# Linear attention and experts on one core: a shared tile for the last 64 keys of two heads, elementwise work moved to GpSimd, and a new order of stages

## The chip, the cores and the metric

The kernel runs on one core of one Trainium2 chip. The metric is the device time of one execution in microseconds (us), from its start to its end. The text names the engines as the profile does: PE is TensorE's matmul, PEld its weight load, DVE VectorE, ACT ScalarE, POOL GpSimd, SP the engine that only issues DMAs.

## The reference

```python
def phi(x):                                   # (4, 8, 576, 64) -> (..., 256)
    proj = np.einsum('bhsd,df->bhsf', x, w_phi)          # 128 features
    proj = proj - np.max(np.abs(proj), axis=-1, keepdims=True)
    return np.concatenate([np.exp(proj), np.exp(-proj)], axis=-1)
q_p, k_p = phi(q), phi(k)
kv = np.einsum('bhsf,bhsd->bhfd', k_p, v)
z = np.sum(k_p, axis=2)
x = np.einsum('bhsf,bhfd->bhsd', q_p, kv) / (np.einsum('bhsf,bhf->bhs', q_p, z)[..., None] + 1e-6)
# x as (2304 tokens, 512); then 4 experts, all tokens through all of them
p = domain_probs / (domain_probs.sum(-1, keepdims=True) + 1e-09)
out = sum(p[:, e:e+1] * (np.maximum(x @ w1[e], 0) @ w2[e]) for e in range(4))   # 512 -> 1024 -> 512
```

## The kernel before

**Attention.** The 4 x 8 heads are worked on as 16 pairs of heads (two heads of one batch element). The features of keys are made with the keys as rows (`proj`, L289), their largest absolute value is subtracted (`proj_sub`), ScalarE takes both exponentials (`k_exp`), and `k_kv` (L358) multiplies them with the values into one bank, 66 columns for each of two heads and two signs, of which 65 are the values and a column of ones (for z). The 576 keys of a head are four tiles of 128 and one of 64. In that last tile each head is a step of its own: of the 128 rows 64 are keys and the other 64 are set to zero after the exponentials; the projection takes both heads side by side (256 columns), and four value products follow. Most matmuls run on numbers split into a high and a low part (fp32r), three products each; `k_kv` runs in plain fp32 at two instructions a product.

For pairs 4 to 15 ("stack") the queries take another path: high and low part stand stacked in the 128 rows (`split_pair`, L195 and L196), `q_proj` (L222) gives the features transposed, `q_max` (L237) takes block maxima on VectorE, which go through `max_d` in DRAM and come back broadcast as `mb`; `q_sub`, `q_exp2` and `q_lo` follow. `q_num` (L440) multiplies with the sums of `k_kv`; the denominators go through DRAM (`den_out`, `den_in`, `den_recip`, `rec_out`), come back broadcast as `rb` (`rec_in`, L479), and `x_mul` (L489) forms the x product. `x_out` splits it for the experts (L382, L502), `x_store` sends what comes later to `xd`.

**Experts.** 16 weight units (an expert's 256 hidden columns each) are run three times. The first time (`first_units`, L716 and `l2_tile`, L680) covers 512 tokens and is interleaved with the attention of pairs 4 to 15. The second and third time (`strassen_unit`, L886) cover 1024 and 768 tokens with seven products in place of eight on half-size blocks; the widths are 512 and 384 columns. These need sums of weight blocks (`s_sums`, L616 to L619, in tile `ws`), split into `s_hi` (L635) and `s_lo` (L643), and sums of token blocks (`x_ops`). Bank A is copied by ScalarE (L832) after the first product and written again by the fourth. Each unit's second layer runs during the next unit, its result added to `out` by VectorE (L690). Weights are loaded into two buffers `wraw` and split (`w_hi` L600, `w_lo` L606).

**What sets the order.** Every stage is a function in one queue that is sorted by a key. The lists `OLD` (pairs 0 to 3) and `NEW` (pairs 4 to 15) give each stage's key; pair i adds 16 i. `tick()` in the expert loops moves a clock forward by one step and emits what is due; `after(steps, fn)` puts something in relative to that clock. So the keys fix the order of instructions on each engine and nothing else: an engine that waits holds up what stands behind it. `FIRST` is the key 85 at which `first_units` starts, `LAST` that of the last `x_out`.

Of the kernel before, what the change touches and what calls it, by code (L numbers as in the profile page):

```python
# [20 lines left out]
def kernel(  # L21
# [17 lines left out]
    P = 128  # L39
# [27 lines left out]
    FETCH = (12, 28, 40, 46)  # L67
    W_WAIT = (5.5, 4.0, 0, 3.5)
# [72 lines left out]
    def load_pair(i, what):  # L141
        s = pairs[i]
        b, hp = divmod(i, NP)
        t0 = b * S
        if what == "kq" and s.stack:
            k = ip_.tile([P, S + 64], F32, name="kr", tag="kr", bufs=2)
            nc.sync.dma_start(k, kq[b, hp][:, 0 : S + 64])
            q = ip_.tile([P, 2 * S], F32, name="qr", tag="kq", bufs=2)
            s.kq = [k, q]
            for r in (0, 64):  # L150
                to = q[r : r + 64].rearrange("p (h s) -> p h s", h=2)
                src = kq[b, hp].rearrange("(h p) s -> p h s", h=2)
                nc.sync.dma_start(to[:, :, S - 64 : S], src[:, :, S : S + 64])
                nc.sync.dma_start(to[:, :, 0 : S - 64], src[:, :, S + 64 : 2 * S])
            return
        if what == "kq":
            s.kq = [ip_.tile([P, 2 * S], F32, name="kq", tag="kq", bufs=2)]
# [12 lines left out]
        t4, t4z = (slice(0, 64), slice(64, P)) if s.stack else (slice(64, P), slice(0, 64))  # L170
        nc.gpsimd.memset(s.v[t4z, 4, :], 0.0)
        for h in range(2):
            src = vsrc[:, h * 64 : (h + 1) * 64]
            dst = s.v[:, :, h * (2 * KW - 64) : h * (2 * KW - 64) + 64]
            nc.sync.dma_start(dst[:, 0:4], src[0:512].rearrange("(t p) d -> p t d", p=P))
            nc.sync.dma_start(dst[t4, 4], src[512:S])
# [10 lines left out]
    def split_pair(i, what):  # L187
# [12 lines left out]
        sl = KSL if what == "k" else QSL  # L200
# [4 lines left out]
        else:  # L205
            both = ip_.tile([P, 2 * S], F32R, name="qhilo", tag="qs", bufs=1)
# [8 lines left out]
    def q_proj(i, part, h):  # L215
# [3 lines left out]
        ps = s.ps[part, h] = ps_att.tile([P, 512], F32, name="projT", tag="att")  # L219
# [48 lines left out]
    def q_exp2(i, part, h):  # L268
# [5 lines left out]
        s.qe[part, h] = exps(src, slice(0, P), 1, 512 if part == 0 else 320, True)  # L274

    def proj(i, what, c):
# [7 lines left out]
        ps = s.ps[what, c] = ps_att.tile([P, 512], F32, name="proj", tag="att")  # L284
        for j in range(2 if c < 2 else 1):
# [8 lines left out]
    def proj_sub(i, what, c):  # L294

        s = pairs[i]
        g = 4 if c < 2 else 2
# [40 lines left out]
    def k_exp(i, c):  # L338
        s = pairs[i]
        t4, t4z = (slice(0, 64), slice(64, P)) if s.stack else (slice(64, P), slice(0, 64))  # L340
        rows, g = (slice(0, P), 4) if c < 2 else (t4, 2)
        d = s.d["k", c][rows, : g * NF]
        s.ke[c] = exps(d.rearrange("p (g f) -> p g f", f=NF), rows, g, NF, False)
        if c == 2:

            nc.gpsimd.memset(s.ke[c][0][t4z, : 2 * g * NF], 0.0)

    def k_kv(i, c):
# [4 lines left out]
        if c == 0:  # L353
            s.kv = ps_kv.tile([P, 512], F32, name="kv", tag="kv")
        for j, t in enumerate(tiles):
            for n in range(4):
                h, e0 = n // 2, (4 * j + n) * NF
                nc.tensor.matmul(  # L358
                    s.kv[:, n * KW : (n + 1) * KW],
# [66 lines left out]
    def q_num(i, part, h):  # L426
# [79 lines left out]
    def x_store(i):  # L506
# [21 lines left out]
        (14.5, q_tr, (1, 0)), (15.2, q_exp, (1, 0)),
        (16, q_lo, (1, 0)),
        (14.55, q_tr, (1, 1)), (15.5, q_exp, (1, 1)),  # L530
        (16.05, q_lo, (1, 1)),
        (18.6, q_num, (0, 0)), (19.9, q_copy, (0, 0)),
        (21.5, q_num, (1, 0)), (22, q_copy, (1, 0)),
        (22.7, q_num, (1, 1)), (23.3, q_copy, (1, 1)),
        (26.2, den_out, ()), (29.8, den_in, ()), (31.2, den_recip, ()), (32.5, rec_out, ()),
        (34.7, rec_in, ()), (36.9, x_mul, ()), (40.5, x_store, ()), (37, x_out, ()),
    )
    NEW = (
        (-22.75, load_pair, ("kq",)),
        (-15.3, load_pair, ("v",)),  # L540
        (-10.5, split_pair, ("k",)),
        (-5.8, split_pair, ("q",)),
        (-0.7, proj, ("k", 0)), (-0.6, proj_sub, ("k", 0)), (2.7, k_exp, (0,)),
        (6.94, k_kv, (0,)),
        (0.52, proj, ("k", 1)), (2.55, proj_sub, ("k", 1)), (4.04, k_exp, (1,)),
        (11.24, k_kv, (1,)),
        (2.8, proj, ("k", 2)), (4.64, proj_sub, ("k", 2)), (8.74, k_exp, (2,)),
        (12.48, k_kv, (2,)), (12.48, kv_hi, ()), (14.03, kv_lo, ()),
        (2.01, q_proj, (0, 0)), (6.04, q_max, (0, 0)),
        (6.24, q_proj, (1, 0)), (6.24, q_max, (1, 0)),  # L550
        (7.19, q_proj, (1, 1)), (7.19, q_max, (1, 1)),
        (9.04, q_maxT, ()), (9.04, q_maxrow, ()), (9.89, q_maxout, ()), (10.44, q_maxin, ()),
        (11.88, q_sub, (0, 0)), (14.38, q_exp2, (0, 0)),
        (13.23, q_sub, (1, 0)), (16.63, q_exp2, (1, 0)),
        (16.45, q_lo, (0, 0)),
        (13.43, q_sub, (1, 1)), (19.9, q_exp2, (1, 1)),
        (17, q_lo, (1, 0)),
        (22.85, q_lo, (1, 1)),
        (24.95, q_num, (0, 0)), (26.65, q_copy, (0, 0)),
        (26.15, q_num, (1, 0)), (26.9, q_copy, (1, 0)),  # L560
        (26.24, q_num, (1, 1)), (26.94, q_copy, (1, 1)),
        (30.24, den_out, ()), (31.27, den_in, ()), (32.22, den_recip, ()), (35.58, rec_out, ()),
        (36.98, rec_in, ()), (37.55, x_mul, ()), (44.4, x_store, ()), (39.37, x_out, ()),
# [45 lines left out]
    def s_sums(n):  # L609
# [5 lines left out]
        sub, tt = ALU.subtract, nc.vector.tensor_tensor  # L615
# [40 lines left out]
    def convert(kind, n, wait):  # L656
# [3 lines left out]
        if kind == "w1" and n >= NU:  # L660
            for o, fn in ((wait[0], s_sums), (wait[0] + 0.5, s_hi), (wait[1], s_lo)):
# [59 lines left out]
    def first_units():  # L721
        pend = []
        for n in range(NU):
# [12 lines left out]
            l1_done(n, W_WAIT[2:])  # L736
# [5 lines left out]
            if pend:  # L742
                l2_done(n - 1, W_WAIT[2:])
# [70 lines left out]
    def strassen_unit(n, x, pend, hooks):  # L814
# [9 lines left out]
        load("w1", n + 2, 1)  # L824
        load("w2", n + 1, 7)
# [24 lines left out]
        def evacuate(i):  # L850
            if i == 0:
                copy("s1", "A")
            elif i == 1:
                after(0.5, add, "u2", "s1", "B")
            elif i == 2:
                copy("s5", "C")
            elif i == 3:
                a = banks["A"][:, :nt]
                relu(0, 0, a)
                after(0.5, lo, 0, 0, a)  # L860
            elif i == 4:
                add("u3", "u2", "D")
                after(1, c22)
                after(2, lambda: nc.scalar.activation(c["c22"], c["c22"], AF.Relu))  # L864
                after(2, lambda: relu(1, 1, c["c22"]))
                after(3, lambda: lo(1, 1, c["c22"], False))
            elif i == 5:
                add("c12", "u2", "C")
                after(0.5, lambda: relu(0, 1, c["c12"]))
                after(1.5, lambda: lo(0, 1, c["c12"]))  # L870
            else:
                add("c21", "u2", "D")
                after(0.5, lambda: relu(1, 0, c["c21"]))
                after(1.5, lambda: lo(1, 0, c["c21"]))
# [23 lines left out]
        l1_done(n, (0.5, 2))  # L898
# [3 lines left out]
        l2_done(n - 1, (0.5, 2))  # L902
# [3 lines left out]
    def second_units(pend):  # L906
        xs, ops = xa, None
        for n in range(NU, 3 * NU):
# [3 lines left out]
            if n == 2 * NU - 1:  # L912
                ops["t4"] = ops["T1"] + ops["t4"]
                for i, name in ((1, "T2"), (2, "t4"), (4, "T3"), (5, "B22"), (6, "T4")):
                    hooks[i] = functools.partial(spread, ops[name], 0.5, 0.5)
            if n == 2 * NU - 2:
                ops = x_ops(xb)
                spread(ops["t"] + ops["t3"], 2, 1.5)
            if n == NU + 3:
                x_load(xb, xb.first, xb.nt)  # L920
                for k in range(NP):
                    after(4 + k, nc.scalar.activation, x0_hi[:, k, : xb.nt], xb.raw[:, k, : xb.nt], AF.Copy)
                    after(
                        6 + k,
# [134 lines left out]
```

## Time and profile before

| what | value |
|---|---|
| median of 3 runs | 991.61 us (987.24 to 992.78) |
| the profiled execution | 991.64 us, span 989.9 us |
| PE busy | 955.9 us (97%), 4883 matmuls |
| DVE busy | 683.8 us (69%) |
| ACT busy | 455.5 us (46%) |
| POOL busy | 542.1 us (55%) |
| mean granted TensorE clock | 0.985 |

The span goes from the first to the last instruction on the core. Busy time of PE is modelled at its ends and counts a pipelined matmul until it is through, so the spacing of starts tells what a matmul costs in a row of them. A wait is named by the engine, the tile it would write, its line, and after the arrow what released it.

### The profile page before, as it was taken

What the parts mean: (1) busy time and instruction counts of PE and PEld (TensorE: products, weight loads), DVE (VectorE), ACT (ScalarE), POOL (GpSimd) and SP (SyncE); (2) the same over time, 40 slices, a digit from 0 to 9 for tenths busy, and PEclk for the clock granted to TensorE, in tenths of its full rate; (3) what the DMA queues carried; (4) which work ended last, traced back from release to release, by engine and by line L of the source; (5) the groups of instructions that cost most, each with busy time, mean ns of one, the idle gap of its engine ahead of it and who ended that gap; (6) DMA issues with size and microseconds to landing.
All of it is one profiled execution on the core that took longest, in us unless ns stands there. A gap on an engine that the chain in (4) does not pass through costs nothing. (4 is left out here: it accounts for less than half of the span.)

```text
span 989.9 us, 13384 instructions
## 1 busy us (share of the span) xinstructions
PE 955.9 (97%) x4883; PEld 824.9 (83%) x4883; DVE 683.8 (69%) x1027; ACT 455.5 (46%) x832; POOL 542.1 (55%) x391
## 2 busy tenths in 40 slices
PE   8998999899999998899999999999989999999998
PEld 7887888788878887688888888888878888888887
DVE  5464776876766778867666666667876667676764
ACT  4675666656656543434333333332434434343441
POOL 3554657575654456655455445544665575655651
PEclk9898999999999999999999999999999999999999
DMA  6444545445543343322121211211132222212111
GB/s 157 127 124 131 136 127 153 122 132 165 142 119 105 130 150 99 102 87 68 43 79 59 64 43 43 63 55 54 43 106 86 65 65 63 86 58 71 64 43 64
DMA packets 74641, 91.42 MB, mean 92 GB/s; under 512 B 35120, under 2 KB 37040, under 8 KB 74576
## 3 DMA queue, kind: packets, MB, share of 16 engines
q1 hardware_dynamic: 74496, 90.55, 31.2%
q8 instruction: 38, 0.62, 0.3%
q14 instruction: 27, 0.22, 0.1%
q10 hardware_dynamic: 80, 0.03, 0.0%
HBM read 83.01 MB, written 7.54 MB: 91 GB/s over the span
## 5 line engine op out<-in xcount | busy, mean ns | idle before, releaser
L690 DVE SCALAR_TENSOR_TENSOR out<-l,pr,out 128x512 f32<-128x512 f32 x270 | 199.7, 746 | 96.2 <-PE l L680 95.1
L680 PE MATMUL l<-w2hi,h_lo 128*128 128x512 f32 x576 | 226.8, 394 | 3.9 <-DVE out L690 3.8
L680 PE MATMUL l<-w2hi,h_hi 128*128 128x512 f32 x576 | 226.3, 393 | 0.0
L680 PE MATMUL l<-w2lo,h_hi 128*128 128x512 f32 x576 | 226.1, 392 | 0.0
L643 POOL TENSOR_TENSOR w1lo<-wraw,w1hi 128x512 fp32r<-128x512 f32 x64 | 79.8, 1267 | 92.9 <-ACT w1hi L635 55.1
L680 PEld LDWEIGHTS l<-w2hi,h_lo 128*128 128x128 f32 x576 | 108.7, 189 | 23.4 <-DVE out L690 5.8
L680 PEld LDWEIGHTS l<-w2hi,h_hi 128*128 128x128 f32 x576 | 108.3, 188 | 23.2
L606 POOL TENSOR_TENSOR w2lo<-wraw,w2hi 128x1024 fp32r<-128x1024 f32 x48 | 116.8, 2434 | 16.5 <-ACT w2hi L600 8.6
L680 PEld LDWEIGHTS l<-w2lo,h_hi 128*128 128x128 f32 x576 | 108.6, 188 | 17.5
L838 ACT ACTIVATE h_hi<-c 128x512 fp32r<-128x512 f32 (+1 forms) x96 | 55.0, 578 | 68.8 <-DVE c L835 67.7
L848 POOL TENSOR_TENSOR c<-u,s 128x512 f32<-128x512 f32 (+1 forms) x32 | 37.2, 1162 | 86.8 <-DVE u L835 86.8
L358 PEld LDWEIGHTS kv<-v,e 128*128 128x128 f32 x640 | 81.1, 199 | 3.4
L358 PE MATMUL kv<-v,e 128*128 128x66 f32 x640 | 79.7, 279 | 0.0
L643 POOL TENSOR_TENSOR s_lo<-ws,s_hi 128x768 fp32r<-128x768 f32 x32 | 59.1, 1846 | 33.6 <-ACT s_hi L635 33.6
L864 ACT ACTIVATE c<-c 128x512 f32<-128x512 f32 (+1 forms) x32 | 18.6, 580 | 125.0 <-POOL c L848 125.0
L332 POOL TENSOR_TENSOR elo<-e,ehi 128x640 fp32r<-128x640 f32 x24 | 42.7, 1780 | 49.5 <-ACT ehi L324 45.0
L845 POOL TENSOR_TENSOR h_lo<-c,h_hi 128x512 fp32r<-128x512 f32 (+1 forms) x32 | 37.6, 1176 | 40.2 <-ACT h_hi L838 40.2
L600 ACT ACTIVATE w2hi<-wraw 128x1024 fp32r<-128x1024 f32 x48 | 50.5, 1052 | 12.8 <-PE l L680 12.7
L635 ACT ACTIVATE s_hi<-ws 128x768 fp32r<-128x768 f32 x32 | 27.1, 848 | 62.6 <-DVE ws L619 62.6
L606 POOL TENSOR_TENSOR w1lo<-wraw,w1hi 128x1024 fp32r<-128x1024 f32 x16 | 40.1, 2506 | 25.1 <-ACT w1hi L600 25.0
L716 PE MATMUL l<-x_hi,w1lo 128*128 128x512 f32 x128 | 52.8, 412 | 1.0 <-ACT x_hi L382 1.0
L886 PE MATMUL A<-x_hi,w1lo 128*128 128x512 f32 (+1 forms) x128 | 47.7, 373 | 6.2 <-ACT s L832 3.7
(161 smaller groups left out, 2226.2 us busy)
## 6 DMA issues: line engine op xcount, KB each, us to landing
wraw<-in_w_dram SPq DMA_DIRECT2D x96, 512.0 KB
mb<-max_d SPq DMA_DIRECT2D x12, 576.0 KB
qr<-in_kq_dram SPq DMA_DIRECT2D x24, 256.0 KB
rb<-rec_d SPq DMA_DIRECT2D x32, 144.0 KB
out_dram<-out SPq DMA_DIRECT2D x18, 256.0 KB
v<-in_v_dram SPq DMA_DIRECT2D x32, 128.0 KB
kr<-in_kq_dram SPq DMA_DIRECT2D x12, 320.0 KB
xd<-rb SPq DMA_DIRECT2D x8, 288.0 KB
```

The costliest lines, as they stand in the source:

```text
L332: engine.tensor_tensor(lo[sl], e[sl], parts[0][sl].bitcast(F32), op=ALU.subtract)
L358: nc.tensor.matmul(s.kv[:, n * KW : (n + 1) * KW], lhsT=e[:, e0 : e0 + NF], rhs=s.v[:, t, h * KW : (h + 1) * KW], start=(c == 0 and j == 0 ...
L600: nc.scalar.activation(hi, raw, AF.Copy)
L606: nc.gpsimd.tensor_tensor(lo, raw, hi.bitcast(F32), op=ALU.subtract)
L643: nc.gpsimd.tensor_tensor(dst, src, hi.bitcast(F32), op=ALU.subtract)
L680: nc.tensor.matmul(ps, lhsT=l[:, f, j * P : (j + 1) * P], rhs=r[:, f, :], start=(f == 0 and k == 0), stop=(f == 1 and k == 2),)
L690: nc.vector.scalar_tensor_tensor(o, ps, p, o, op0=ALU.mult, op1=ALU.add)
L716: nc.tensor.matmul(banks[n, f], lhsT=l[:, ksl], rhs=r[:, k, :], start=(k == 0 and j == 0), stop=(k == NP - 1 and j == 2),)
L838: nc.scalar.activation(h[b][0][:, f, :nt], src, AF.Relu)
L845: nc.gpsimd.tensor_tensor(dst, src, hi.bitcast(F32), op=ALU.subtract)
L848: nc.gpsimd.tensor_tensor(temp("c22"), c["u3"], c["s5"], op=ALU.add)
L886: nc.tensor.matmul(ps, lhsT=l[:, k * P : (k + 1) * P], rhs=r[:, k, :], start=(k == 0 and j == 0 and not again), stop=(k == 1 and j == 2), ...
```

## The change

It touches four things. In pairs 4 to 15 the last 64 keys of both heads share one tile of 128 rows (head 0 above, head 1 below). These keys are no longer loaded into `k` but, by two more DMAs, as 128 more columns of the stacked `q` tile, once in the rows of the high part and once in those of the low part; `proj` takes the tile with the stacked weights in two matmuls of 128 columns, and the values of the tile are block-diagonal (two blocks of zeros), so that `k_kv` makes two products of 132 columns in place of four of 66. The columns of the sums change their order from head, sign to sign, head. Second, `x_mul` runs on GpSimd in place of VectorE, in all 16 pairs. Third, so do the four weight sums of `s_sums`. Fourth, nearly all keys of the two lists change, and in the second units the waits are given for each stretch of units (`S_...`, `XB_...`, `W_WAIT_A`) in place of fixed numbers. The diff, cut to its core:

```diff
-    FETCH = (12, 28, 40, 46)
-    W_WAIT = (5.5, 4.0, 0, 3.5)
+    FETCH = (12.4, 27.45, 41.5, 43)
+    W_WAIT = (3.6, 1.4, 0, 2.85)
+    W_WAIT_A = (0, 3.5, 0.4, 2)
+    S_LOAD = (1, 5.35)
+    S_EV = (0.5, 0.5, 1, 2, 2, 3, 0.5, 1.5, 0.5, 1.5)
+    S_EV_A = (0.35, 1.3, 1, 2, 2, 3, 1.3, 1.5, 0.5, 0.7)
+    S_DONE = (0.5, 1, 3.5, 0.5, 1.45)
+    S_DONE_A = (0.5, 1, 3.5, 0.5, 2)
+    S_DONE_B = (0, 1, 5, 0.5, 2.4)
+    S_DONE_C = (0, 1, 5, 0.5, 2)
+    XB_HOOK = (0, 1.3, 0.5, 1.3, 0.35, 0.5)
+    XB_SUM = (0.4, 2.85)
+    XB_X = (4.4, 6)
...
-            k = ip_.tile([P, S + 64], F32, name="kr", tag="kr", bufs=2)
-            nc.sync.dma_start(k, kq[b, hp][:, 0 : S + 64])
-            q = ip_.tile([P, 2 * S], F32, name="qr", tag="kq", bufs=2)
+            k = ip_.tile([P, S - 64], F32, name="kr", tag="kr", bufs=2)
+            nc.sync.dma_start(k, kq[b, hp][:, 0 : S - 64])
+            q = ip_.tile([P, 2 * S + P], F32, name="qr", tag="kq", bufs=2)
...
+                nc.sync.dma_start(tail, src[:, :, S - 64 : S])
...
+        if s.stack:
+            t4 = [slice(0, 64), slice(64, P)]
+            nc.gpsimd.memset(s.v[0:64, 4, KW : 2 * KW], 0.0)
+            nc.gpsimd.memset(s.v[64:P, 4, 0:KW], 0.0)
...
-            t = ip_.tile([P, 2 * S], F32R, name="qs", tag="qs", bufs=1)
+            t = ip_.tile([P, 2 * S + P], F32R, name="qs", tag="qs", bufs=1)
...
+        if s.stack and c == 2:
+            for k in (1, 0):
+                nc.tensor.matmul(ps[:, 0:NF], lhsT=s.q[:, 2 * S :], rhs=wst[k], start=(k == 1), stop=(k == 0))
+            return
...
-        g = 4 if c < 2 else 2
+        g = 4 if c < 2 else 1 if s.stack else 2
...
-        rows, g = (slice(0, P), 4) if c < 2 else (t4, 2)
+        rows, g = (slice(0, P), 4) if c < 2 else (slice(0, P), 1) if s.stack else (slice(64, P), 2)
...
-        if c == 2:
-            nc.gpsimd.memset(s.ke[c][0][t4z, : 2 * g * NF], 0.0)
+        if c == 2 and not s.stack:
+            nc.gpsimd.memset(s.ke[c][0][0:64, : 2 * g * NF], 0.0)
...
+        if s.stack and c == 2:
+            for sg in range(2):
+                nc.tensor.matmul(
+                    s.kv[:, 2 * sg * KW : 2 * (sg + 1) * KW], lhsT=e[:, sg * NF : (sg + 1) * NF],
+                    rhs=s.v[:, 4, :], start=False, stop=True, skip_group_check=True,
+                )
+            return
...
-            nc.vector.tensor_tensor(s.xt[sl], s.nd[sl, h, :], s.rb[sl], op=ALU.mult)
+            nc.gpsimd.tensor_tensor(s.xt[sl], s.nd[sl, h, :], s.rb[sl], op=ALU.mult)
...
-        (30.24, den_out, ()), (31.27, den_in, ()), (32.22, den_recip, ()), (35.58, rec_out, ()),
-        (36.98, rec_in, ()), (37.55, x_mul, ()), (44.4, x_store, ()), (39.37, x_out, ()),
+        (29.06, den_out, ()), (29.77, den_in, ()), (31.42, den_recip, ()), (33.91, rec_out, ()),
+        (38.29, rec_in, ()), (39.91, x_mul, ()), (44, x_store, ()), (40.15, x_out, ()),
...
-        sub, tt = ALU.subtract, nc.vector.tensor_tensor
+        sub, tt = ALU.subtract, nc.gpsimd.tensor_tensor
...
-        l1_done(n, (0.5, 2))
+        l1_done(n, done[:3])
...
-        l2_done(n - 1, (0.5, 2))
+        l2_done(n - 1, done[3:])
```

The lines of keys are from `NEW`; the other keys of both lists change in the same way. In `OLD`, `x_mul` goes from 36.9 to 38.07 and `x_out` from 37 to 39.52, so that pair 3's `x_out` (16 x 3 more) comes after `FIRST`.

## Rows read from the trace of the kernel before

**Rows 1.** The windows view, one row for each stage; columns after the span: busy us.
```profile
core 0: us, PE busy (x) PEld busy (x) DVE busy (x) ACT busy (x) POOL busy (x), PEclk, DMA share, GB/s
0.00:85.00 85.00, 74.55 (x465) 67.83 (x466) 46.38 (x89) 51.40 (x106) 39.20 (x49) 0.92 0.50 131
85.00:391.50 306.50, 293.63 (x1708) 256.63 (x1707) 223.07 (x332) 180.69 (x329) 178.33 (x114) 0.99 0.47 134
391.50:433.80 42.30, 38.06 (x157) 30.11 (x158) 35.51 (x44) 17.22 (x30) 27.28 (x19) 0.97 0.27 88
433.80:719.00 285.20, 285.20 (x1258) 235.83 (x1257) 195.35 (x283) 104.62 (x178) 148.16 (x101) 1.00 0.19 58
719.00:742.70 23.70, 21.16 (x95) 18.13 (x94) 17.14 (x24) 8.35 (x17) 14.36 (x12) 0.93 0.34 111
742.70:990.00 247.30, 243.25 (x1207) 216.37 (x1205) 166.30 (x259) 93.27 (x174) 134.79 (x100) 1.00 0.21 67
```
**Rows 2.** Waits of TensorE, 85 to 391.5 us: total us, times, longest us.
```profile
PE num L440 <- DVE bm L237: 5.5, 6, 2.3
```
**Rows 3.** Timeline of VectorE around 214 us: start, us, instruction and count.
```profile
213.06 2.80 DVE L489 TENSOR_TENSOR rb<-nd,rb 64x576 f32<-64x576 f32 x2
215.89 1.11 DVE L237 TRANSPOSE_TENSOR_REDUCE bm<-projT 128x16 f32<-128x512 f32 x2
```
**Rows 4.** Waits of TensorE, 391.5 to 742.7 us.
```profile
PE A L886 <- ACT s L832: 3.7, 2, 2.5
PE A L886 <- DVE h_lo L703: 2.5, 1, 2.5
```
**Rows 5.** Timeline of ScalarE around 826 us; in brackets the idle time before.
```profile
825.54 0.85 ACT L635 ACTIVATE s_hi<-ws 128x768 fp32r<-128x768 f32 x1 [2.17 <-DVE ws L619]
826.30 0.46 ACT L832 COPY s<-A 128x384 f32<-128x384 f32 x1
```
**Rows 6.** Timeline of TensorE around 222 us.
```profile
221.49 1.89 PE L358 MATMUL kv<-v,e 128*128 128x66 f32 x16
223.19 0.47 PE L680 MATMUL l<-w2hi,h_lo 128*128 128x512 f32 x1
```
**Rows 7.** Timeline of TensorE around 11 us.
```profile
10.51 1.08 PE L289 MATMUL proj<-wbd,kq 128*128 128x256 f32 x4
11.43 0.60 PE L408 MATMUL dT<-ident,d 128*128 128x128 f32 x4
11.86 0.34 PE L358 MATMUL kv<-v,e 128*128 128x66 f32 x2
```
**Rows 8.** Timeline of TensorE around 208 us.
```profile
208.44 0.28 PE L289 MATMUL proj<-wbd_hi,klo 128*128 128x256 f32 x1
...
208.80 0.40 PE L716 MATMUL l<-x_hi,w1lo 128*128 128x512 f32 x1
```
**Rows 9.** Groups by line and shape, whole run: busy us, mean ns | idle before.
```profile
L196 POOL TENSOR_TENSOR qs<-qr,qs 64x1152 fp32r<-64x1152 f32 x12 | 31.8, 2650 | 8.5 <-PE num L440 3.4 <-ACT qs L195 3.0 <-issue 1.6
```
**Rows 10.** Timeline of the SP queue around 213 us.
```profile
212.97 0.61 SPq L154 DMA_DIRECT2D qr<-in_kq_dram  x1
219.00 0.33 SPq L255 DMA_DIRECT2D max_d<-mrow  x1
```
**Rows 11.** Groups of VectorE, 742.7 to 990 us.
```profile
L618 DVE TENSOR_TENSOR ws<-wraw 128x256 f32<-128x256 f32 x14 | 20.2, 1444 | 0.0
...
L619 DVE TENSOR_TENSOR ws<-wraw,ws 128x256 f32<-128x256 f32 x14 | 13.4, 955 | 0.0
...
L617 DVE TENSOR_TENSOR ws<-ws,wraw 128x256 f32<-128x256 f32 x14 | 5.9, 425 | 0.5
L616 DVE TENSOR_TENSOR ws<-wraw 128x256 f32<-128x256 f32 x14 | 5.8, 416 | 0.0
```
**Rows 12.** Groups of GpSimd, 742.7 to 990 us.
```profile
L845 POOL TENSOR_TENSOR h_lo<-c,h_hi 128x384 fp32r<-128x384 f32 x15 | 15.4, 1024 | 17.9 <-ACT h_hi L838 17.9
...
L643 POOL TENSOR_TENSOR w1lo<-wraw,w1hi 128x256 fp32r<-128x256 f32 x14 | 12.9, 921 | 0.0
```
**Rows 13.** The windows view for one unit of 384 tokens.
```profile
805.32:820.98 15.66, 15.66 (x79) 13.97 (x78) 10.98 (x17) 6.38 (x13) 9.46 (x7) 1.00 0.21 68
```

More of the change, by code (lines that the diff above doesn't have):

```diff
@@ L156, in load_pair @@
         if what == "kq":
-            s.kq = [ip_.tile([P, 2 * S], F32, name="kq", tag="kq", bufs=2)]
+            s.kq = [ip_.tile([P, 2 * S + P], F32, name="kq", tag="kq", bufs=2)]
             parts = ((0, 2 * P), (2 * P, 4 * P)) if i == 0 else ((0, 4 * P),)
@@ L199, in split_pair @@
         raw = s.kq[0]
-        sl = KSL if what == "k" else QSL
+        sl = slice(0, S - 64) if s.stack else KSL if what == "k" else QSL
         n = sl.stop - sl.start
@@ L205, in split_pair @@
         else:
-            both = ip_.tile([P, 2 * S], F32R, name="qhilo", tag="qs", bufs=1)
+            both = ip_.tile([P, 2 * S + P], F32R, name="qhilo", tag="qs", bufs=1)
             hi, lo = both[:, :n], both[:, S : S + n]
@@ L218, in q_proj @@
         s = pairs[i]
-        ps = s.ps[part, h] = ps_att.tile([P, 512], F32, name="projT", tag="att")
+        ps = s.ps[part, h] = bank(i, ps_l1, "l1", "projT")
         for k in (1, 0):
@@ L273, in q_exp2 @@
             src = s.d["q"][:, h, 256:S].unsqueeze(1)
-        s.qe[part, h] = exps(src, slice(0, P), 1, 512 if part == 0 else 320, True)
+        s.qe[part, h] = exps(src, slice(0, P), 1, 512 if part == 0 else 320, s.split_num)
     def proj(i, what, c):
@@ L563 @@
-        (36.98, rec_in, ()), (37.55, x_mul, ()), (44.4, x_store, ()), (39.37, x_out, ()),
+        (-23.15, load_pair, ("kq",)),
+        (-14.46, load_pair, ("v",)),
+        (-6.83, split_pair, ("k",)),
+        (-6.49, split_pair, ("q",)),
+        (-1.17, proj, ("k", 0)), (-0.67, proj_sub, ("k", 0)), (1.05, k_exp, (0,)),
+        (7.09, k_kv, (0,)),
+        (-0.1, proj, ("k", 1)), (2.4, proj_sub, ("k", 1)), (7.84, k_exp, (1,)),
+        (12.44, k_kv, (1,)),
+        (3.05, proj, ("k", 2)), (3.84, proj_sub, ("k", 2)), (7.64, k_exp, (2,)),
@@ new lines @@
+        (12.48, k_kv, (2,)), (12.48, kv_hi, ()), (12.53, kv_lo, ()),
+        (1.39, q_proj, (0, 0)), (6.04, q_max, (0, 0)),
+        (6.24, q_proj, (1, 0)), (6.64, q_max, (1, 0)),
+        (7.04, q_proj, (1, 1)), (7.19, q_max, (1, 1)),
+        (9.04, q_maxT, ()), (9.04, q_maxrow, ()), (10.59, q_maxout, ()), (10.84, q_maxin, ()),
+        (12.03, q_sub, (0, 0)), (14.38, q_exp2, (0, 0)),
+        (13.18, q_sub, (1, 0)), (16.93, q_exp2, (1, 0)),
+        (16.6, q_lo, (0, 0)),
+        (12.48, q_sub, (1, 1)), (19.9, q_exp2, (1, 1)),
@@ L660, in convert @@
         if kind == "w1" and n >= NU:
-            for o, fn in ((wait[0], s_sums), (wait[0] + 0.5, s_hi), (wait[1], s_lo)):
+            wait = (wait[0], wait[0] + 0.5, wait[1]) if len(wait) == 2 else wait
+            for o, fn in zip(wait, (s_sums, s_hi, s_lo)):
                 later(max(clock.key, LAST + XA_LATE + 1) + o * clock.step, functools.partial(fn, n))
@@ L735, in first_units @@
                 tick()
[L736 removed]
+            l1_done(n, W_WAIT_A[:2] if n >= NU - 2 else W_WAIT[2:])
             if n:
@@ L853, in evacuate @@
             elif i == 1:
-                after(0.5, add, "u2", "s1", "B")
+                after(ev[0], add, "u2", "s1", "B")
             elif i == 2:
@@ L921, in second_units @@
                 for k in range(NP):
-                    after(4 + k, nc.scalar.activation, x0_hi[:, k, : xb.nt], xb.raw[:, k, : xb.nt], AF.Copy)
+                    after(XB_X[0] + k, nc.scalar.activation, x0_hi[:, k, : xb.nt], xb.raw[:, k, : xb.nt], AF.Copy)
                     after(
-                        6 + k,
+                        XB_X[1] + k,
                         lambda k=k: nc.vector.tensor_tensor(
```

111 lines of the change are left out of this document (49 added, 62 removed).

## The prediction

> **What bounds the kernel now.** I read the busy time of each engine by stage first [rows 1]. The stages are cut at what the trace shows: up to 85 us attention alone, to 391.5 us attention interleaved with the first expert units, to 433.8 us the start of the second units, to 719 us units of 512 tokens, to 742.7 us the change to 384 tokens, and from there units of 384. The reader is to see that TensorE is the bound nearly everywhere and how little idle time it has: 10.5 us before 85, 12.9 us in the interleaved stage (306.50 less 293.63), 4.2 us in the next (42.30 less 38.06), none in 433.8 to 719, 2.5 us around 719, and 4.1 us after, which I take for the tail behind the last matmul. The granted clock is below 1.00 only in stages with idle time. So the time falls in two ways: TensorE gets less to do, or the idle stretches close. 433.8 to 719 can give nothing.
>
> Second, what those stretches wait for. In the interleaved stage the largest item is the numerator matmul waiting for VectorE's block maximum, 5.5 us in six waits [rows 2]. The timeline of VectorE in one such place shows why [rows 3]: two x products take 2.80 us, from 213.06, and the block maximum that TensorE wants starts at 215.89, straight after them. From 391.5 to 742.7 two product-A matmuls wait 3.7 us for ScalarE's copy of A, and one 2.5 us for VectorE's h_lo [rows 4]. Behind that copy is a chain: ScalarE's s_hi waits for VectorE's last weight sum, and the copy stands behind it in ScalarE's order. In a steady unit of 384 the chain ends so: s_hi waited 2.17 us and started at 825.54, the copy at 826.30 [rows 5].
>
> **The change, part by part.** *Tail tile, values.* Each of 12 pairs loses half of its last four value products. Each of those is two instructions (fp32), so 8 become 4, twice as wide (132 columns for 66). Sixteen of the old kind start between 221.49 and 223.19, 0.106 us each [rows 6]. The trace has no 132-column one. From below it costs what a 66-column one does, 0.106: saved 4 x 0.106 = 0.42 us a pair. From above, four fp32 instructions of 256 columns take 10.51 to 11.43, 0.23 each [rows 7], so 132 columns in proportion 0.119: saved 8 x 0.106 less 4 x 0.119 = 0.37. I take 0.37, the nearer kind.
>
> *Tail tile, projection.* Three matmuls of 256 columns, 208.44 to 208.80, 0.36 us [rows 8], become two of 128. Half of 0.12 each is the lower bound, 0.06. The nearest row is the transpose of 128 columns: four between 11.43 and 11.86, 0.108 each [rows 7]. I take 0.108: saved 0.36 less 0.22 = 0.14 us; by the lower bound 0.24. Together 0.51 us a pair (0.66 at most), times 12 is 6.1 us (7.9). Pair 4 does this before 85 us, where TensorE has idle time to lose it in, so **5.6 us**.
>
> *The smaller work around it.* One memset of GpSimd a pair goes, the maximum and subtraction of the tail halve, ScalarE's exponentials of the tail have half the columns on twice the rows; the q split grows from 1152 to 1280 columns, the k split shrinks from 640 to 512. None of these engines is the bound, and their idle time hides it, so nothing is booked; uncovered, the q split would cost a ninth of 2.65 us, 0.3 us a pair [rows 9]. Two more DMAs a pair stand in SP's queue, 0.61 us each: the block-maximum store behind them would be 1.2 us late if SP were full, but SP is idle from 213.58 to 219.00 there [rows 10].
>
> *x products to GpSimd.* VectorE loses 2.80 us a pair just ahead of the block maximum. GpSimd has no such row; half of its 64x1152 subtraction, 2.65 us, gives 1.33 each [rows 9], 2.65 a pair. GpSimd is busy 178.33 of 306.50 us in that stage [rows 1]; a dozen pairs add some 32, 69% in all. What the move adds is a wait: on GpSimd the product stands in line behind the reciprocals' broadcast, with the low parts of the exponentials and splits queued behind it, and the numerator and projections wait for those. Bounds: at best the 5.5 us of waits go; at worst they come back as waits on GpSimd, nothing gained. I take **4.5 us**: the longest wait is 2.3 us against 2.80 removed, so all could close, and a new one or two are likely to remain.
>
> *Weight sums to GpSimd.* In a unit of 384, four sums leave VectorE, 3.2 us together [rows 11]. GpSimd's nearest row is a subtraction of the same 128x256 shape, 0.921 us [rows 12], so 3.7 us a unit. GpSimd is busy 9.46 of 15.66 us there [rows 13], and h_lo waits 17.9/15 = 1.2 us on ScalarE with nothing between [rows 12]: 9.46 + 3.7 + 1.2 = 14.4, which fits. The sums need nothing but the raw weights, so GpSimd can start them when it is through with the unit's h_lo; s_hi and the copy behind it come no later. In steady units TensorE has no idle time to win, so the gain is zero; it is paid for if the 14.4 grows past 15.66. The dearest row for a sum is VectorE's 1.444, while another of the same shape takes 0.416 [rows 11]: at 1.444 on GpSimd the unit would need 16.4.
>
> The Trainium skill explains such a pair of rows: "SBUF — State Buffer", section "Who interferes with whom", says that a VectorE instruction with two SBUF inputs and a GpSimd instruction that reads SBUF block each other for a whole instruction. By this rule a sum on GpSimd is free of the blocking and the forecast stands; were 1.444 what the operation itself costs, the sum would end 11 us later (rival C).
>
> *The two junctions* (391.5 and 719) lose 4.2 and 2.5 us idle, plus clock: a granted 0.97 over 42.3 us and 0.93 over 23.7 us is 1.3 and 1.7 us. Together 9.7 us. Sums off VectorE and new hooks may close part; but GpSimd, busy 27.28 of 42.30 in the first [rows 1], gets some three sets of sums, 11 us, and becomes nearly full. Bounds 0 and 9.7 gained; I take **2.5**, because the copy of A still stands behind s_hi and s_hi behind the sums.
>
> *Stages placed anew.* In 85 to 391.5 the order of matmuls against the other engines changes; the rows can't price it. Bounds: all 12.9 us close, or as many again open. I book no more than the 4.5 above. Before 85, pair 3's x product costs 2 x 1.33 ahead of the first expert matmuls that read it; its output is placed after three groups of them, which is cover. I book zero.
>
> Sum: 991.64 (the profiled execution, whose span is 989.9 with 1.7 outside it, and which is at the median of the runs, 991.61) less 5.6, 4.5 and 2.5 is **979 us**.
>
> **The rivals.** *A: only the work comes off.* VectorE's waits close and waits on GpSimd open in their place (the x product behind its broadcast), the junctions stay: 991.6 less 5.6 = 986, 982 to 990. For it: TensorE's waits add up from small ones of many kinds. Against: the largest kind has one cause, and that is removed.
>
> *B: the new order closes nearly all idle time.* 12.9, 4.2, 2.5 and the 3 us of clock, with 5.6 of work: 991.6 less 28 = 963. For it: nothing but order holds these waits. Against: each has another releaser.
>
> *C: GpSimd becomes the bound in the units of 384, slower.* The point from which it decides: a sum of (15.66 - 1.2 - 9.46)/4 = 1.25 us. At VectorE's dearest 1.444 each of 14 such units ends 4 x 0.19 us late, 11 us; GpSimd that late gives back no waits elsewhere either, so 991.6 less 5.6 plus 11 = 997. For it: 14.4 of 15.66 leaves little. Against: GpSimd's own row of this shape is 0.921, measured beside the very VectorE sums that leave. The Trainium skill's "GPSIMD Engine Reference", section "Engine selection", speaks for C: it advises VectorE for elementwise work, GpSimd being about twice as slow with two inputs; twice VectorE's mean of 0.81 would be 1.6 a sum and some 1007 us in all.
>
> *D: the wide value product costs twice the narrow one,* so that nothing is saved on it: 12 x 0.37 back, 983. Against it: 256 columns take 0.23, so 132 can hardly take 0.21.
>
> **How the numbers follow.** The forecast 979 (970 to 984) has 0.55, A 0.20, B 0.10, C 0.10, D 0.05. About half a percent, 5 us, is what a measurement can tell from no change: the runs shown go from 987.24 to 992.78. Faster means under 986.7. The forecast, B, D and most of A lie there, less a little for an order that misses: 0.79. Same: the rest of A and C's mild end, 0.12. Slower: the rest of C and an order that opens new waits, 0.09. The range from 964 to 990 leaves out half of B, most of C and the new waits.
>
> **What would show it.** Right: the tail's value products at 0.106 to 0.12 us with half as many; VectorE's block maximum no longer behind x products and the wait for it under 2 us in all; GpSimd some 13 us busy in a unit of 384, and that unit still 15.6 to 15.7 us; idle time in 85 to 391.5 of 6 to 10 us. Wrong: waits of TensorE on GpSimd's low parts above 5 us in that stage (A), a unit of 384 longer than 16 us (C), idle time under 4 us there (B), or a stage before 85 that grows or shrinks by more than 3 us, which I left at zero.

## The result, and the profile after

The changed kernel takes 966.79 us (median of 4 runs, 966.39 to 967.29) where the kernel before took 990.31 beside it (4 runs, 987.24 to 992.78): a ratio of 0.9764, 95% interval 0.9734 to 0.9795. It is faster by 23.5 us; 12.6 were forecast. The profiled execution is 967.29 us with a span of 965.5.

The windows view of the kernel after, with the columns of [rows 1]. Its stages are cut at five events: the first expert product, and the first product A of the first, third, 17th and 18th of the second units.

```profile
0.00:80.43 80.43, 69.32 (x448) 62.35 (x449) 38.83 (x79) 48.55 (x100) 45.91 (x53) 0.95 0.52 136
80.43:371.71 291.28, 286.16 (x1664) 250.49 (x1664) 197.23 (x311) 182.91 (x335) 208.24 (x144) 1.00 0.50 140
371.71:413.98 42.27, 38.81 (x157) 30.89 (x158) 26.94 (x32) 18.12 (x32) 37.32 (x31) 0.92 0.32 99
413.98:699.60 285.62, 285.62 (x1261) 236.57 (x1260) 160.82 (x227) 104.77 (x178) 190.36 (x156) 1.00 0.18 58
699.60:718.77 19.17, 18.66 (x91) 16.25 (x90) 13.66 (x19) 8.13 (x17) 15.92 (x16) 1.00 0.40 132
718.77:965.50 246.73, 242.96 (x1207) 217.45 (x1205) 125.92 (x203) 92.58 (x173) 169.28 (x154) 1.00 0.20 67
```

The first cut of [rows 1] lies 2.9 us behind its event and the cut at 719 lies 0.7 ahead. At exactly these events the kernel before has 82.09 us in the head (the stage up to the first expert product), 309.43 in the interleaved stage, then 42.25, 285.90, 22.97 and 247.20. Its first two:

```profile
0.00:82.09 82.09, 72.13 (x454) 66.06 (x455) 43.77 (x85) 48.52 (x100) 37.64 (x48) 0.92 0.50 130
82.09:391.52 309.43, 296.06 (x1719) 258.42 (x1718) 225.71 (x337) 183.56 (x335) 179.92 (x115) 0.99 0.47 134
```

So the head gave 1.7 us, the interleaved stage 18.2, the first junction (371.71 to 413.98) nothing, the units of 512 tokens 0.3, the second junction (699.60 to 718.77) 3.8, and the units of 384 0.5: together the 24.4 us by which the span fell. TensorE's idle time in the interleaved stage fell from 13.37 to 5.12 us. GpSimd took what VectorE lost: 208.24 busy us there, and 37.32 of 42.27 in the first junction.

The waits of TensorE in the interleaved stage:

```profile
PE l L715 <- DVE out L725: 3.1, 2, 1.7
PE l L751 <- POOL x_lo L536: 0.8, 1, 0.8
PE l L751 <- ACT x_hi L416: 0.4, 1, 0.4
PE maxT L264 <- DVE bm L256: 0.2, 1, 0.2
```

The numerator's 5.5 us of waits for the block maximum [rows 2] are gone, and no wait on GpSimd's low parts of the exponentials has come for them. The waits from 371.7 to 718.77, which answer to [rows 4]:

```profile
PE C L923 <- POOL B22lo L823: 2.3, 1, 2.3
PE C L923 <- ACT s L869: 1.2, 1, 1.2
PE A L923 <- POOL w1lo L677: 0.6, 1, 0.6
PE A L923 <- ACT s L869: 0.5, 1, 0.5
```

Here the waits changed hands: 6.2 us on ScalarE's copy and VectorE's low part (9.3 with the smaller waits of that stretch) have become 4.6, the longest on GpSimd.

TensorE's timeline at two places, the tail's value products and its projection, against [rows 6, 8]:

```profile
96.80 0.39 PE L392 MATMUL kv<-v,e 128*128 128x66 f32 x2
97.02 0.67 PE L383 MATMUL kv<-v,e 128*128 128x132 f32 x4
97.44 0.48 PE L751 MATMUL l<-x_hi,w1lo 128*128 128x512 f32 x1
...
127.86 0.33 PE L308 MATMUL proj<-wst,qs 128*128 128x128 f32 x2
128.03 0.45 PE L715 MATMUL l<-w2hi,h_lo 128*128 128x512 f32 x1
```

Read start to start, not by the duration: two instructions of 66 columns take 0.22 us, four of 132 take 0.42. Either kind costs 0.11 each. The two projection matmuls take 0.17 together.

The groups of GpSimd in the units of 384 (busy us, mean ns | idle before), against [rows 12]:

```profile
L651 POOL TENSOR_TENSOR ws<-ws,wraw 128x256 f32<-128x256 f32 x13 | 12.2, 942 | 1.0
...
L677 POOL TENSOR_TENSOR w1lo<-wraw,w1hi 128x256 fp32r<-128x256 f32 x14 | 10.4, 745 | 0.0
L653 POOL TENSOR_TENSOR ws<-wraw,ws 128x256 f32<-128x256 f32 x14 | 10.4, 744 | 0.0
L652 POOL TENSOR_TENSOR ws<-wraw 128x256 f32<-128x256 f32 x13 | 9.6, 737 | 0.0
L650 POOL TENSOR_TENSOR ws<-wraw 128x256 f32<-128x256 f32 x13 | 9.6, 737 | 0.0
```

The four sums take 942 + 744 + 737 + 737 = 3160 ns a unit, and one such unit by the windows view, against [rows 13]:

```profile
781.36:797.00 15.64, 15.64 (x80) 14.06 (x79) 8.04 (x13) 6.37 (x13) 11.93 (x12) 1.00 0.22 69
```

### The profile page after: what moved, and what is told of

Its sections match the earlier page's. It is cut to its first block, busy times and chain, and to the rows that moved or that the text cites. A ratio compares the mean times of both kernels' runs of the same rounds, so it can differ in the third digit from the quotient of the medians.

```text
span 965.5 us, 13190 instructions
## 1 busy us (share of the span) xinstructions
PE 941.5 (98%) x4823; PEld 814.0 (84%) x4823; DVE 563.4 (58%) x867; ACT 455.1 (47%) x832; POOL 667.0 (69%) x551
## 4 chain that ended last, share of the span: by engine, by line
PE 77%; POOL 6%; DMA 6%; DVE 4%; ACT 2%; issue 2%; SPq 2%; POOLq 0%; ACTq 0%
PE l L715 36%; PE C L923 8%; PE D L923 8%; PE A L923 8%; PE l L751 5%; PE B L923 4%; PE num L474 3%; PE kv L392 3%; PE proj L314 1%; DVE dq L285 1%; DMA mb<-max_d 1%; DMA wraw<-in_w_dram 1%; POOL w2lo L640 1%; POOL rb L523 1%; DMA qr<-in_kq_dram 1%
## 5 line engine op out<-in xcount | busy, mean ns | idle before, releaser
L357 POOL TENSOR_TENSOR elo<-e,ehi 128x640 fp32r<-128x640 f32 x24 | 40.1, 1673 | 52.9 <-ACT ehi L349 47.8
L392 PEld LDWEIGHTS kv<-v,e 128*128 128x128 f32 x544 | 65.5, 193 | 5.1 <-ACT e L345 2.4
L392 PE MATMUL kv<-v,e 128*128 128x66 f32 x544 | 66.0, 274 | 3.1 <-ACT e L345 1.5
L677 POOL TENSOR_TENSOR w1lo<-wraw,w1hi 128x512 fp32r<-128x512 f32 x64 | 65.2, 1040 | 0.0
L872 DVE TENSOR_TENSOR u<-s,B 128x512 f32<-128x512 f32 (+1 forms) x32 | 19.9, 621 | 64.4 <-ACT s L869 30.7
L523 POOL TENSOR_TENSOR rb<-nd,rb 64x576 f32<-64x576 f32 x32 | 46.7, 1458 | 8.0 <-DMA rb<-rec_d 6.7
```

What stands on the lines that cost most here:

```text
L357: engine.tensor_tensor(lo[sl], e[sl], parts[0][sl].bitcast(F32), op=ALU.subtract)
L392: nc.tensor.matmul(s.kv[:, o * KW : (o + 1) * KW], lhsT=e[:, e0 : e0 + NF], rhs=s.v[:, t, h * KW : (h + 1) * KW], start=(c == 0 and j == 0 ...
L523: nc.gpsimd.tensor_tensor(s.xt[sl], s.nd[sl, h, :], s.rb[sl], op=ALU.mult)
L677: nc.gpsimd.tensor_tensor(dst, src, hi.bitcast(F32), op=ALU.subtract)
```

## The experiments

The edits are named T (the tail tile), X (x products on GpSimd), W (weight sums on GpSimd), K (the keys of both lists, with `FETCH` and `W_WAIT`) and S (the waits given by stretch in the second units). No kernel leaves work out. A gain in us is the ratio's, of 990 us, unless medians are named; the two can differ by some 2 us (T alone is 7.1 faster by the ratio, 5.4 by the medians). Stage times are of each kernel's profiled execution, between the events above, and such a time varies for the same instructions. `ws` below changes nothing in the head, and in the interleaved stage at most the last weight sums. Its head:

```profile
0.00:79.59 79.59, 70.01 (x455) 63.29 (x455) 43.75 (x85) 48.40 (x100) 37.62 (x48) 0.96 0.52 135
```

That is 2.5 us less in the head, at a granted clock of 0.96 for 0.92, and its interleaved stage is 306.03 us, 3.4 less. In these two stages a difference of less than some 3 us is not told apart by one execution each.

### One part alone

T alone is the diff's hunks from `load_pair` to `k_kv`, with the new order of columns in `q_num`; all else is as before.

> The kernel before with the shared tail tile alone. Theory 1 (each gain is the part's own, as the prediction summed them): 5.6 to 6.1 us faster, value products of 132 columns at 0.11 to 0.12 us each. Theory 2 (the new order is what closes the idle time and the parts only fit into it): the matmul time falls by as much, but idle time of the old order opens in its place, so 0 to 4 us faster.

It takes 980.67 us, ratio 0.9928 (0.9897 to 0.9958): 7.1 us of 990. The interleaved stage is 299.96 us, TensorE busy in 288.44 of it against 296.06 before, idle in 11.52 against 13.37. Its largest wait is unchanged, the numerator for the block maximum:

```profile
PE num L462 <- DVE bm L244: 5.6, 5, 2.3
```

So T takes off work; that it closes any wait is not shown.

X alone:

```diff
-            nc.vector.tensor_tensor(s.xt[sl], s.nd[sl, h, :], s.rb[sl], op=ALU.mult)
+            nc.gpsimd.tensor_tensor(s.xt[sl], s.nd[sl, h, :], s.rb[sl], op=ALU.mult)
```

> The kernel before with the x products on GpSimd alone, keys as before. Theory 1: VectorE loses 2.8 us a pair ahead of the block maximum, the 5.5 us of waits for it go and more of the interleaved stage's 12.9 idle us with them: 4 to 12 us faster. Theory 2: under the old keys GpSimd waits behind the broadcast, and the time is within 3 us of before.

It takes 992.26 us, ratio 1.0059 (1.0026 to 1.0092): X alone loses 5.8 us. Its first two stages:

```profile
0.00:89.17 89.17, 76.64 (x454) 69.57 (x455) 41.49 (x79) 48.63 (x101) 46.54 (x54) 0.88 0.45 120
89.17:394.08 304.91, 295.11 (x1718) 260.10 (x1717) 191.45 (x311) 182.70 (x335) 205.86 (x138) 0.99 0.47 134
```

The interleaved stage gains 4.5 us, the very figure of the forecast, though against `ws` it would be 1.1. The head loses 7.1 and the first junction 3.4. GpSimd's timeline in the head shows one cause, and TensorE's the price (the last line):

```profile
56.71 3.14 POOL L489 TENSOR_TENSOR rb<-nd,rb 64x576 f32<-64x576 f32 x2
60.59 1.55 POOL L502 TENSOR_TENSOR x_lo<-rb,x_hi 128x512 fp32r<-128x512 f32 x2 [0.74 <-ACT x_hi L382]
62.10 1.53 POOL L209 TENSOR_TENSOR klo<-kr,khi 128x640 fp32r<-128x640 f32 x1
63.57 0.51 POOL L346 MEMSET e<- 64x512 f32 x1
...
64.14 1.98 PE L358 MATMUL kv<-v,e 128*128 128x66 f32 x8 [2.38 <-POOL e L346]
```

The two x products hold GpSimd for 3.14 us; the low parts of x and k follow, and a memset of half a microsecond stands last. TensorE's value products wait 2.38 us for it. The granted clock of the head is 0.88 here and 0.92 before, and TensorE's busy time is 76.64 us against 72.13 for the same work: 4.5 of the 7.1 us are busy time, 2.6 idle time. In the interleaved stage the largest wait is this:

```profile
PE num L440 <- POOL elo L332: 4.7, 3, 2.0
```

5.5 us of waits on the block maximum have become 4.7 on GpSimd's low part: the mechanism of rival A.

K alone changes the two lists, `FETCH` and `W_WAIT`, as in the diff.

> The kernel before with only the keys of the two attention lists and of the first units' weight loads and splits from after. Theory 1 (moving work off VectorE closes the idle time): within 3 us of before. Theory 2 (the order closes it): the interleaved stage loses 8 to 12 us, and with the start 8 to 14 us in all.

980.66 us, ratio 0.993 (0.9904 to 0.9955), 6.9 us faster with no operation moved to another engine. The interleaved stage falls to 299.37 us (5.94 idle), 10.1 less. The numerator's 5.5 us of waits for the block maximum are gone from it, though the x products are still VectorE's. VectorE's timeline there shows a reason, against [rows 3]:

```profile
212.31 1.51 DVE L237 TRANSPOSE_TENSOR_REDUCE bm<-projT 128x16 f32<-128x512 f32 x3 [0.56 <-ACT dq L234]
...
216.18 1.53 DVE L489 TENSOR_TENSOR rb<-nd,rb 64x576 f32<-64x576 f32 x2
```

The block maxima now stand ahead of the x products. In `NEW` the product of pair i had the key 37.55, just ahead of the block maxima of pair i + 2 (6.04 to 7.19, plus 32); with 39.91 it comes behind them. (Other keys change too, so that this one does it is argued.) The head grows by 3.5, its clock at 0.88, all of it in TensorE's busy time (76.23 us against 72.13).

W alone:

```diff
-        sub, tt = ALU.subtract, nc.vector.tensor_tensor
+        sub, tt = ALU.subtract, nc.gpsimd.tensor_tensor
```

> The kernel before with only the four weight sums on GpSimd, waits of the second units as before. Theory 1: the sums fit in GpSimd's idle time, units stay at 15.66 and 20.4 us, the change at 719 us loses 1 to 3 us: 0 to 3 us faster. Theory 2 (the sums need the new waits): s_lo and w2lo come late at the old places, and the time is 0 to 10 us longer.

982.65 us, ratio 0.9969 (0.9932 to 1.0006): not told apart from no change. But by stages two things stand out: the second junction falls from 22.97 to 18.63 us, the first grows from 42.25 to 45.02, where TensorE waits 2.8 us for GpSimd's w2lo.

### One part taken out of the kernel after

Out of the changed kernel, one part each goes back to what it was: X, K, W, S and T, the same lines as above (`no_w` keeps the new waits, `no_s` has the old ones).

> The kernel after with the x products back on VectorE. Alone under the old keys the move cost 0.6%. Theory 1: the product on GpSimd is worth its 4.5 us where the keys leave room for it, so without it the after is 4 to 10 us longer and waits for the block maximum come back. Theory 2 (the order alone closes the idle time, the engine of the x product does not matter): within 2 us of after.

> The kernel after with the old keys of the attention lists and of the first units' loads. Theory 2: it loses 12 to 18 us against after, 979 to 985, because the x product on GpSimd then stands as badly as in the run with it alone. Theory 1: it loses 5 to 7 us, what the keys gave alone, 972 to 974.

> The kernel after with the four weight sums back on VectorE. Theory 1 (parts add): 3 us longer than after, 969 to 970. Theory 2 (the new waits of the second units are cut for sums on GpSimd): 5 to 10 us longer, with product A waiting for the copy of A in many units.

> The kernel after with the fixed waits of the second units. If the change at 719 us is closed by moving the sums, the stage stays at its 19.2 us and the time within 1 us of after; if the new hooks and waits close it, 3 to 5 us of it come back: 970 to 972.

> The kernel after without the shared tail tile. By TensorE's work alone it is 6 to 7 us longer than after, 973 to 974. If the smaller work of the tile on VectorE and GpSimd counts as well, as the 7.1 us of the run with it alone allow, 8 to 12 us, 975 to 979.

| without | median us | ratio to before (95%) | slower than after, by the medians | by the ratios |
|---|---|---|---|---|
| X | 972.17 | 0.9834 (0.9814 to 0.9855) | 5.4 | 6.9 |
| K | 981.91 | 0.9920 (0.9895 to 0.9946) | 15.1 | 15.4 |
| W | 1010.09 | 1.0202 (1.0171 to 1.0233) | 43.3 | 43.4 |
| S | 968.72 | 0.9805 (0.9782 to 0.9827) | 1.9 | 4.1 |
| T | 974.69 | 0.9824 (0.9783 to 0.9866) | 7.9 | 5.9 |

X, which loses 5.8 us alone, is worth 5.4 under the new keys: its sign depends on K. But the waits for the block maximum that were expected back without it do not come back: in `no_x` the interleaved stage is 293.27 us with 4.94 idle, where the kernel after has 291.28 with 5.12. So X closes no idle time there under the new keys, and what its 5.4 us are made of is not shown. Without K the interleaved stage is 301.47 us with 14.28 idle, as much idle time as before; so the idle time closed by the change is closed by the order.

S shows in the first junction: 45.18 us without it, with 2.1 us of TensorE's waits on GpSimd's w2lo, against 42.27 with it. The second junction is no longer without it (18.63), so moving the sums is what shortens that one.

The 43 us without W are far more than the 5 to 10 expected, and of another kind. Most of them fall in the units of 384, 254.19 us for 14 of them against 218.99; 7.3 more fall in the first junction. GpSimd's timeline there, VectorE's and ScalarE's, three parts in one:

```profile
838.55 2.62 POOL L640 TENSOR_TENSOR w2lo<-wraw,w2hi 128x1024 fp32r<-128x1024 f32 x1 [3.52 <-ACT w2hi L634]
...
838.50 0.41 DVE L650 TENSOR_TENSOR ws<-wraw 128x256 f32<-128x256 f32 x1
838.95 2.51 DVE L651 TENSOR_TENSOR ws<-ws,wraw 128x256 f32<-128x256 f32 x1
841.38 1.51 DVE L652 TENSOR_TENSOR ws<-wraw 128x256 f32<-128x256 f32 x1
842.81 0.95 DVE L653 TENSOR_TENSOR ws<-wraw,ws 128x256 f32<-128x256 f32 x1
...
843.79 0.84 ACT L669 ACTIVATE s_hi<-ws 128x768 fp32r<-128x768 f32 x1 [4.24 <-DVE ws L653]
844.54 0.46 ACT L869 COPY s<-A 128x384 f32<-128x384 f32 x1
```

The sums start on VectorE 1.3 us after the unit's product A, as they did before. But by the new waits GpSimd's w2lo is issued earlier and runs beside them, and the second sum takes 2.51 us, where it took 0.42 before [rows 11]; the four take 5.3 us from first start to last end. s_hi waits 4.24, the copy of A stands behind it, and the later product A that needs this copy waits for it, 23.7 us in 13 such waits. S is fitted to W: with the sums on VectorE it does harm.

### Is it the list of the first pairs, or of the rest?

`old_first` is the changed kernel with the `OLD` list of before, `old_rest` with the `NEW` list of before.

> The kernel after with the old keys for pairs 0 to 3 alone. If the x product on GpSimd is what makes the start long (89 us under old keys with it), the first expert product comes 6 to 7 us later and the time is 972 to 974. If the start's keys do not matter, within 1.5 us of after.

> The kernel after with the old keys for pairs 4 to 15 alone. If the rest of the 15 us that the old keys cost is here, the interleaved stage is 8 to 11 us longer, 975 to 978, with low parts on GpSimd as TensorE's releaser; if the order of these pairs does not matter, within 2 us of after.

With the old `OLD`: 973.09 us, ratio 0.9818 (0.9772 to 0.9864), some 6 us lost, but not where they were expected: the head is 82.49 us and the interleaved stage 294.22, 2.1 and 2.9 more than in the kernel after. With the old `NEW`: 994.41, ratio 1.0031 (1.0002 to 1.0060), worse than with both old (981.91). Here the head is 96.50 us, 16.1 more, and the interleaved stage 302.38, 11.1 more. The lists are not two terms of a sum. In the head of `old_rest` two single waits of TensorE lead, 6.2 us for VectorE's `d` and 5.1 for its `kvhi` (the waits on GpSimd's low parts, which were expected to lead, are 3.3); which keys of the one list come late for the other was not tried.

### X and K together; X with the reciprocals' keys alone; W with S

`xk` has X and K. `x_recip` is X alone with only the keys from `den_out` to `x_out` taken from the change, so that the product comes when its broadcast has landed. `ws` has W and S with `W_WAIT_A`.

> The kernel before with the x products on GpSimd and the new keys, no shared tile, sums on VectorE. If the new keys are what turns the x product from 5.8 us lost into 5 us gained, this is 10 to 13 us faster than before. If the parts merely add, 1 us faster.

> The run with the x products on GpSimd alone, and of the new keys only those from the denominators' store to x_out. If the loss comes from GpSimd standing at the x product until the broadcast has landed, the waits of the x product for that DMA fall from 16.4 us to under 6 and the time is 4 us or more below that run, at or below before. If it comes from the order of the low parts and splits around it, within 2 us of that run.

> The kernel before with the weight sums on GpSimd and the new waits of the second units. If the new waits repair the 2.8 us that the sums on GpSimd cost at the junction after 391 us, that stage is back at 42 us and the time 4 to 6 us below before; if that repair hangs on the new keys, as with the sums alone, 2 to 3.5 us.

X and K together: 973.99 us, ratio 0.9838 (0.9782 to 0.9895), 16.0 us faster, where X alone is 5.8 slower and K alone 6.9 faster. The head is 78.49 us, the interleaved stage 296.01 with 2.97 idle. `x_recip` takes 1003.27 us, ratio 1.0137 (1.0089 to 1.0185). GpSimd hardly stands there any more waiting for the broadcast's DMA (16.4 us in x_alone, 2.5 here), and yet it is 8 us slower than x_alone by the ratios; so taking that wait away does not by itself win back what X costs, and the theory falls. Other waits have grown instead, those on VectorE's accumulation from 2.2 us to 10.4, and those on the memset from 3.2 to:

```profile
PE kv L358 <- POOL e L346: 5.4, 3, 3.2
```

In the changed kernel, by GpSimd's timeline at the corresponding place, that memset has passed the low part of k:

```profile
56.17 1.54 POOL L536 TENSOR_TENSOR x_lo<-rb,x_hi 128x512 fp32r<-128x512 f32 x2 [0.74 <-ACT x_hi L416]
57.65 0.52 POOL L370 MEMSET e<- 64x512 f32 x1
58.13 1.26 POOL L228 TENSOR_TENSOR klo<-kr,khi 128x512 fp32r<-128x512 f32 x1
```

and from pair 4 on there is none, since the tail tile needs no zeros there. (`xk`, which has the new keys and not the tail tile, waits 1.0 us for it.)

W and S together: 982.42 us, ratio 0.9935 (0.9899 to 0.9971), 6.4 us faster. The first junction, 45.02 us with W alone, is 41.27, without the wait on w2lo: the new waits of S repair what W costs there, under the old keys too.

### Could both sides of the first junction be had?

`mix` keeps the sums of the first junction on VectorE, since GpSimd is nearly full there:

```diff
-        sub, tt = ALU.subtract, nc.gpsimd.tensor_tensor
+        sub, tt = ALU.subtract, (nc.vector if n < NU + 2 else nc.gpsimd).tensor_tensor
```

> The kernel after with the weight sums of the first two second units back on VectorE, where GpSimd had no idle time from 362 to 391 us and product C waited 2.3 us for its B22lo. If that is the cause of what is left at this junction, the stage of 42.3 us loses 2 to 4 us, 963 to 965; if VectorE is as late there, within 1 us of after.

969.38 us, ratio 0.9772 (0.9735 to 0.9808), not better than the kernel after. GpSimd falls to 32.61 busy us in that stage and the wait for B22lo is gone, but TensorE now waits for VectorE's accumulation at one place there, and the stage is 42.60 us:

```profile
PE l L715 <- DVE out L725: 4.4, 1, 4.4
```

## Why the prediction was right or wrong

The direction holds, but 966.79 us lies below the forecast's own range, 970 to 984, and only inside the wide one, 964 to 990: the change gained nearly twice the forecast. By stages, forecast against measured: the interleaved stage 10.1 (5.6 + 4.5) and 18.2; the junctions 2.5 and 3.8; the head 0 and 1.7; the steady units 0 and 0.8. Of the 12 us by which the span fell beyond the forecast, 8 are in the interleaved stage.

**The step that failed is "Stages placed anew": "I book no more than the 4.5 above."** The order was taken as a cost that the rows can't price and set to zero, though TensorE's idle time there, 12.9 us, was bounded by rows. K alone takes 10.1 us off that stage, X alone 4.5, both together 13.4 (309.43 to 296.01): the keys add 9 to the 4.5 that were booked. With X in both, they take idle time from 9.81 us in x_alone to 2.97 in xk; the largest part are the 4.7 us of waits on GpSimd's low part, which xk does not have. In xk TensorE's recorded busy time also fell, by 3.0 us against before, for the same work and at a granted clock of 0.99 in both; what that is made of the runs don't show.

**The 4.5 of the x products had the wrong mechanism, and its number came out by luck.** It was booked because the product leaves VectorE, which stood ahead of the block maximum. X alone does end those waits and opens 4.7 us on GpSimd in their place, nearly the worse of the step's two bounds. K alone ends them with the product still on VectorE, by the order, and in `no_x` they stay away. By the kernel's text the numerator does not need the maximum that it waits for: `q_num` of pair i comes behind the block maxima of pair i + 1 and takes one of the three `att` banks, which their `projT` holds until it is read. So it is a matter of order; that the bank is what it waits for is argued from the text, no run tests it.

**The head at zero was right only by the same keys.** The step said that pair 3's x product has three groups of matmuls as cover before its output is needed. The product's own readers had that cover; those behind it in GpSimd's order had none: the memset, half a microsecond of work, costs 2.38 us in one wait of x_alone. What is queued behind the product was named for the low parts of exponentials and splits, not for the memset, and not for the head. The head is 89.17 us with X alone, 85.60 with K alone, 78.49 with both, and 80.43 in the kernel after, whose 1.7 us less than before are within what `ws` shows for the same instructions. The wait is shown to be a part of X's 7.1 us. The larger part, 4.5, is busy time at a lower granted clock (0.88 against 0.92); whether the waits brought the clock down is not shown.

**The tail tile's work: right, a little small.** 6.1 us in all, 5.6 outside pair 4, were forecast. The spacing gives 0.42 us for the values (132 columns at the lower bound of their cost, where 0.37 was taken) and 0.36 less 0.17 = 0.19 for the projection, where 0.14 was taken: 0.61 us a pair, 7.3 in all. T alone gave 7.1, and the run without it loses 7.9 by the medians, 5.9 by the ratios; TensorE's busy time in the interleaved stage fell by 7.6 with T alone and by 6.9 from xk to the kernel after. Rival D is refuted: 132 columns cost what 66 do.

**The weight sums: right that the steady units gain nothing, and that they hold.** A unit of 384 went from 15.66 to 15.64 us. GpSimd's 11.93 busy us are less than the 13.2 forecast (9.46 + 3.7): the sums took 3.16 us, and the low part of the same shape fell from 921 to 745 ns once VectorE's sums were gone. Rival C, which needed 1.25 us a sum, is refuted, at 0.74 to 0.94. The Trainium skill's "SBUF — State Buffer", section "Who interferes with whom", has VectorE instructions with two SBUF inputs and GpSimd's reads block each other; the trace agrees on both sides, with the 176 ns that the low part got back and with the sum of 2.51 us on VectorE when it ran beside GpSimd's w2lo. The factor of two in the Trainium skill's "GPSIMD Engine Reference", section "Engine selection", agrees with the trace for a VectorE that runs alone (0.74 against 0.42), but the comparison that decided here is with VectorE's mean of 0.81 in this company [rows 11].

ScalarE's s_hi no longer waits, as its timeline in that unit shows against [rows 5], where it had waited 2.17 us:

```profile
783.66 0.83 ACT L669 ACTIVATE s_hi<-ws 128x768 fp32r<-128x768 f32 x1
784.39 0.45 ACT L869 COPY s<-A 128x384 f32<-128x384 f32 x1
```

**The junctions: the reason given for 2.5 was half right.** That "the copy of A still stands behind s_hi and s_hi behind the sums" holds no more: the sums are done when s_hi comes up. That freed the second junction, 3.8 us, and W alone shows the cause (22.97 to 18.63). Not all of it is the sums': T alone and X alone, with the sums on VectorE, have 21.42 and 21.44 us there at a granted clock of 1.00, where before has 0.93, so some 1.5 us are the clock and 2.3 to 2.8 the sums. "GpSimd, busy 27.28 of 42.30 in the first [rows 1], gets some three sets of sums, 11 us, and becomes nearly full" was right: 37.32 of 42.27 us, a wait of 2.3 on its B22lo, and no gain (42.25 to 42.27). There the sums alone would have cost 2.8 us, and S gives them back. `mix` shows that moving the sums back there only changes whom TensorE waits for.

**Rival A is what X does alone; rival B, at 963, came nearest in time**, though the interleaved stage keeps 5.12 us idle, between the 6 to 10 that were to show the forecast right and the 4 that were to show B, and the first junction 3.46. Left open: which single keys do it. Both lists are needed together and one at a time loses; the new place of the x product is the likeliest cause for the end of the largest wait, but no run moved that key alone.

## What to carry to other kernels

Where every engine takes its work in a fixed order, an operation moved to an idle engine has no price of its own: the same line cost 5.8 us under the old order and gave 5.4 under the new, and what to look for is the short instruction that now stands behind it (here a memset of 0.5 us). And before an operation is moved off an engine because it delays a short one there, see whether it can stand behind that one on the same engine: here the new order ended the same waits with the product still on VectorE. So bound the order by the idle time of the bounding engine in that stage, and give the end where it closes a real chance. Moving elementwise work off an engine also speeds up what ran beside it, which the rows of the busy case hide.

## What the runs showed of the hardware that was not expected

An fp32 matmul instruction of 132 columns starts its successor as early as one of 66 (0.42 us for four, 0.22 for two), and two fp32r matmuls of 128 columns cost 0.17 us where one of 256 cost 0.12. On VectorE the same 128x256 sum took from 0.41 to 2.51 us depending on what ran beside it; on GpSimd, once they all ran there, 0.74 to 0.94. And the same instructions up to the first expert product took 79.59 us in one execution, at a granted clock of 0.96, and 82.09 in another, at 0.92.
